# GpSimd in place of VectorE for the first rounding step of w_gate and w_val, one tile ahead

## The chip, the cores and the metric

The kernel runs on one NeuronCore of a Trainium2 chip. The metric is device time in microseconds, from the first to the last instruction of the program plus what the launch adds around it; lower is better. Five engines work side by side, each through its own queue in program order: TensorE (PE, with its weight loads as PEld), VectorE (DVE), ScalarE (ACT), GpSimd (POOL) and SyncE (SP). In this kernel SP does nothing but issue DMA transfers.

## The reference

Three steps in float32 follow one another.

```
attention: 8 batches x 8 heads, 576 tokens in chunks of 64, head size 64
           P = softmax(q k^T / 8) within a chunk;  x = P v         -> x: 4608 tokens x 512
GLU:       gate = sigmoid(x @ w_gate);  val = x @ w_val            w_gate, w_val: 512 x 1536
           y = (gate * val) @ w_out                                w_out: 1536 x 512
activation MLP: h = y @ w_in;  g = h if h >= 1, 0 if h <= -1, else (h+1)^2/4
           out = g @ w2_out                                        2048 wide inside
```

## The kernel before, in words

Every float32 product is formed from three matmuls on rounded halves: an operand is split into a high part, rounded to TensorE's `fp32r` form, and a low part, the remainder. A tile of weights therefore has to be converted and split before it can be used. The weights arrive as 64-bit words (two 32-bit words per value), and the conversion of one tile of 128 x 512 values, named by its key (`("g", 0)`, `("v", 0)`, `("g", 1)`, ...; k0, k1, k2, ... below), runs over three engines:

- `w_load` (SP, L103): the transfer from memory into the tile `raw`.
- `w_low` (L112, a `tensor_scalar` on DVE): the low words are scaled and clamped in place, the first step.
- `w_bits`: a `scalar_tensor_tensor` on DVE (L118) joins sign bits and low word; an ACT step (L122) scales the high word.
- `w_split`: `w_join` on DVE (L126), the high part on ACT (L135), and the remainder on POOL (L136, `w<-raw,w`). After that TensorE can use the tile `w`.

There are 24 tiles of this kind, k0 to k23 (`gate` and `val` in turn, 12 each). The tiles of the later weights pass through `w_low`, `w_bits` and `w_join` too, but are then combined further.

The tokens are worked through in nine blocks of 512. First comes `first_block()`: the attention of block 0, for four pairs of heads p0 to p3, with an order written out by hand in the string `ORDER`. Its letters are the steps: t (transposes of q and k), s (scores on PE at L321, row maxima and subtraction on DVE at L331 and L333, exponential on ACT at L338), n (row sums at L343 to L346 on DVE and the scaling of P on POOL, L351), p (the transpose PT of P on PE at L357 and its copy on ACT at L360), o (the product with v at L367, then x with its low part on ACT at L375 and DVE at L380), and c, which takes the next piece of weight conversion from a list named `pieces`. The loads are issued in the order of the string `LOADS`, further weight loads as pieces are done.

After that, block 0 and every later block go through the projection loop: 24 slots a block, a slot being one projection of 12 matmuls (L459 to L461, `pr<-x,w`). Around these slots the function `at(slot, priority, ...)` places all other work, and `emit(slot)` writes it into the queues in order of slot and priority. During block 0 the slots carry the conversion of the remaining weight tiles (in slot n: the split of the tile used in slot n + 4, the first and second step of the tile used in slot n + 5, the load of the tile for slot n + 9) and the attention of block 1, a new pair of heads every five slots. The first step of that attention is t, which here is two transposes on DVE (L304); its scores on PE (L321) stand one slot later. After block 0 no w_gate or w_val tile is converted any more.

Of the kernel before, what the change touches and what calls it, by code (L numbers as in the profile page):

```python
# [29 lines left out]
def kernel(  # L30
# [15 lines left out]
    nc = tc.nc  # L46
# [31 lines left out]
    def f32(t):  # L78
        return t.bitcast(F32)
# [6 lines left out]
    keys = [(kind, f) for f in range(F1) for kind in "gv"]  # L86
# [4 lines left out]
    def words(raw):  # L91
        return lambda i, dt: raw.bitcast(dt).rearrange("p (n w) -> p n w", w=2)[:, :, i]

    def w_load(key):
        kind, f = key
        sl = slice(f * P, (f + 1) * P)
        if kind in "gv" and keys.index(key) < 8:
            raw = wp.tile([P, 512], I64, tag="w", name="raw")
        else:
            raw = pool["raw"].tile([P, 512], I64, tag="raw", name="raw", bufs=pool["nraw"])  # L100
        src = {"g": w_gate, "v": w_val, "o": w_out, "i": w2_in, "p": w2_out}[kind]
        if kind in "gvi":
            nc.sync.dma_start(  # L103
                out=raw.rearrange("p (k f) -> p k f", f=P), in_=src[:, sl].rearrange("(k p) f -> p k f", p=P)
            )
        else:
            nc.sync.dma_start(out=raw, in_=src[sl, :])
        raws[key] = raw

    def w_low(key):  # L110
        word = words(raws[key])
        nc.vector.tensor_scalar(  # L112
            out=word(0, I32), in0=word(0, U32), scalar1=2.0**-29, scalar2=7.0, op0=ALU.mult, op1=ALU.min
        )

# [77 lines left out]
    def s_prep(kind, k):  # L193

        half_ = (F1 if kind == "o" else F2) // 2
        a, b = (kind, k), (kind, k + half_)
        return [
            (0, w_load, a), (0, w_load, b), (4, w_low, a), (4, w_bits, a), (5, w_low, b), (5, w_bits, b),
            (6, w_join, a), (6, w_join, b), (7, s_sums, kind, k), (8, s_split, kind, k, 0), (8, s_split, kind, k, 1),
            (9, s_split, kind, k, 2), (10, s_spool, kind, k, 0), (10, s_spool, kind, k, 1),  # L200
            (10, s_split, kind, k, 3), (11, s_spool, kind, k, 2), (12, s_spool, kind, k, 3),
        ]
# [179 lines left out]
    def first_block():  # L382
        ft = ps.tile([P, BS], F32, tag="b5", name="fill")

        def fill(n):
            for _ in range(n):
                nc.tensor.matmul(ft, lhsT=z[:, :P], rhs=z, start=True, stop=True)

        pieces = []
        for i in range(NW + 1):  # L390
            pieces.append((w_low, keys[i]))
            pieces.append((w_bits, keys[i]))
            if i:
                pieces.append((w_split, keys[i - 1]))
        nl = [0]

        def wl(n):
            for _ in range(n):
                w_load(keys[nl[0]])
                nl[0] += 1  # L400

        def conv(n):
            while n and pieces:
                fn, key = pieces.pop(0)
                fn(key)
                if fn is w_split and nl[0] < NW + 5:
                    wl(1)
                n -= fn is not w_low

        z = pool["sg"].tile([P, BS], F32R, tag="sg", name="z", bufs=4)  # L410
        nc.vector.memset(f32(z), 0.0)
        kv_["ident"] = cp.tile([P, P], F32, name="ident")
        make_identity(nc, kv_["ident"])
        a = Whole(
            0, [["b0", "b2", "b4"], "b1", "b3", "b6", "b7", "b5"],
            lambda nm: wp.tile([P, 2, BS], F32, tag="w", name=nm), "MVMT",
        )
        for c in LOADS:
            if c == "w":
                wl(1)  # L420
            elif c in "0123":
                a.load(int(c))
            else:
                a.v_load("abcd".index(c))
        for c in ORDER.split():
            if c[0] == "f":
                fill(int(c[1:]))
            elif c[0] == "c":
                conv(int(c[1:]))
            else:  # L430
                for fn in {"t": "t", "s": "sme", "n": "nw", "p": "pc", "o": "oxl"}[c[0]]:
                    getattr(a, fn)(int(c[1:]))
        conv(99)
        assert nl[0] == NW + 5, nl
# [317 lines left out]
    def at(slot, prio, fn, *args):  # L752
        order[0] += 1
        ev.setdefault(int(slot // 1), []).append((slot % 1, prio, order[0], fn, args))
# [15 lines left out]
    NW = 4  # L770
    for i, key in enumerate(keys):
        if i >= NW + 5:
            at(i - NW - 5, 2.5, w_load, key)
        if i > NW:
            at(i - NW - 1, 6, w_low, key)
            at(i - NW - 1, 6, w_bits, key)
        if i >= NW:
            at(i - NW, 5.5, w_split, key)
# [17 lines left out]
    for i in range(FIRST):  # L796
        key, name = ("o", 0, i), ("o", 0, 1, i)
# [52 lines left out]
    with tc.manual_schedule():  # L850
# [13 lines left out]
        pool["nraw"] = 8  # L864
        open_pool("u", "au")
        first_block()
        for t in range(-6, 0):
            emit(t)
# [52 lines left out]
```

## Time and profile before

| what | value |
|---|---|
| median of 3 runs | 1714.94 us (1713.28 to 1716.34) |
| the profiled execution | 1715.51 us, of it span 1713.7 us |
| PE busy in the span | 1668.6 us, 97% |
| DVE, ACT, POOL busy | 1171.4, 863.9, 833.8 us (68%, 50%, 49%) |
| conversion of w_gate and w_val | from 7.9 us (first L112) to 120.7 us (end of the last L136) |

The span is the time from the first to the last recorded instruction; the execution's own time is 1.8 us longer. A row of a timeline gives the start, the duration, engine, line, operation, written and read tiles, and in brackets how long the engine stood idle before and for whom. Rows joined by "x2" or "x32" are several equal instructions in one. A row of waits gives waiting line, the engine and line waited for, microseconds in total, number of waits, longest.

### The profile page before, as it was taken

Reading aid. Unit: us, or ns where it says so; the run is one execution under the profiler, and the core shown is the slowest. Engines: PE = TensorE matmul, PEld = TensorE weight load, DVE = VectorE, ACT = ScalarE, POOL = GpSimd, SP = SyncE. Lnnn points to the kernel's source line nnn. Section 1 sums busy time; section 2 is a strip of 40 time slices with the busy share of each in tenths; the row PEclk is TensorE's granted clock in tenths of the full one; section 3 lists DMA queues with packets and bytes.
Section 4 is the critical chain, followed back from the end, with each engine's and each line's share of the span. In section 5 each row is a group of like instructions: output and inputs, shape, how many; then the busy total and the mean of one; then the engine's idle time right before and its main releaser. Section 6 shows DMA issues by size and latency. Waiting matters only on the chain.

```text
span 1713.7 us, 29607 instructions
## 1 busy us (share of the span) xinstructions
PE 1668.6 (97%) x10658; PEld 1528.4 (89%) x10658; DVE 1171.4 (68%) x1727; ACT 863.9 (50%) x1560; POOL 833.8 (49%) x758
## 2 busy tenths in 40 slices
PE   6899999999999999999999999999999999999996
PEld 5678888888888888899999989999999999999996
DVE  5874555555555541297777767888787888887975
ACT  4664454445444541155555555555554545455542
POOL 2432444433434340177777754444350477677774
PEclk7999999999999999999999999999999999999998
DMA  8856768777668656634644653423329764455442
GB/s 203 218 134 163 213 172 239 228 201 235 212 200 230 212 188 231 217 122 141 226 142 148 246 221 133 155 104 148 148 107 340 281 215 116 107 156 154 115 111 38
DMA packets 386723, 307.11 MB, mean 179 GB/s; under 512 B 268944, under 2 KB 299664, under 8 KB 386576
## 3 DMA queue, kind: packets, MB, share of 16 engines
q1 hardware_dynamic: 386576, 305.22, 57.8%
q8 instruction: 84, 1.38, 0.3%
q14 instruction: 63, 0.52, 0.1%
HBM read 179.83 MB, written 125.30 MB: 178 GB/s over the span
## 4 chain that ended last, share of the span: by engine, by line
PE 86%; DVE 7%; SPq 2%; ACT 1%; issue 1%; POOL 1%; DMA 1%; ACTq 0%; DVEq 0%; POOLq 0%
PE P L460 17%; PE P L461 17%; PE P L459 16%; PE pr L459 11%; PE pr L461 11%; PE pr L460 11%; DVE z L492 3%; PE O L367 2%; PE S L321 1%; SPq L284 1%; DVE z L503 1%; PE PT L357 1%; POOL z L503 1%; DVE raw L118 1%; DVE raw L126 0%
## 5 line engine op out<-in xcount | busy, mean ns | idle before, releaser
L503 POOL TENSOR_TENSOR z<-z 128x384 fp32r<-128x384 f32 x308 | 357.2, 1184 | 313.3 <-ACT z L496 309.1
L460 PE MATMUL P<-z,w 128*128 128x384 f32 x1344 | 451.5, 336 | 8.4 <-DVE z L503 4.2
L459 PE MATMUL P<-z,w 128*128 128x384 f32 x1344 | 449.8, 335 | 0.8 <-ACT z L496 0.8
L461 PE MATMUL P<-z,w 128*128 128x384 f32 x1344 | 449.6, 335 | 0.0
L459 PE MATMUL pr<-x,w 128*128 128x512 f32 x864 | 347.8, 403 | 0.0
L461 PE MATMUL pr<-x,w 128*128 128x512 f32 x864 | 338.0, 391 | 0.0
L460 PE MATMUL pr<-x,w 128*128 128x512 f32 x864 | 337.4, 391 | 0.0
L496 ACT ACTIVATE z<-z 128x384 fp32r<-128x384 f32 x420 | 205.1, 522 | 180.3 <-DVE z L492 105.8
L878 DVE TENSOR_TENSOR sg<-pr,sg 128x512 f32<-128x512 f32 x108 | 74.6, 691 | 313.0 <-PE pr L461 144.5
L460 PEld LDWEIGHTS P<-z,w 128*128 128x128 f32 x1344 | 252.8, 188 | 13.6 <-POOL z L503 7.7
L503 POOL TENSOR_TENSOR op<-in,op 128x384 fp32r<-128x384 f32 x168 | 190.8, 1155 | 148.2 <-ACT op L496 147.8
L459 PEld LDWEIGHTS P<-z,w 128*128 128x128 f32 x1344 | 252.7, 188 | 1.3 <-ACT z L496 1.1
L461 PEld LDWEIGHTS P<-z,w 128*128 128x128 f32 x1344 | 252.8, 188 | 0.0
L459 PEld LDWEIGHTS pr<-x,w 128*128 128x128 f32 x864 | 162.6, 188 | 35.4
L461 PEld LDWEIGHTS pr<-x,w 128*128 128x128 f32 x864 | 162.5, 188 | 35.3
L460 PEld LDWEIGHTS pr<-x,w 128*128 128x128 f32 x864 | 163.0, 189 | 31.4
L496 ACT ACTIVATE op<-in 128x384 fp32r<-128x384 f32 x252 | 128.5, 524 | 112.8 <-PE P L461 60.7
L875 ACT ACTIVATE sg<-pr 128x512 f32<-128x512 f32 x108 | 64.5, 597 | 233.5 <-PE pr L461 226.7
L492 DVE TENSOR_TENSOR z<-z 128x384 f32<-128x384 f32 x200 | 169.9, 900 | 5.8 <-POOL z L503 5.8
L460 PE MATMUL P<-op,w 128*128 128x384 f32 x504 | 168.5, 334 | 0.1
L459 PE MATMUL P<-op,w 128*128 128x384 f32 x504 | 168.4, 334 | 0.0
L461 PE MATMUL P<-op,w 128*128 128x384 f32 x504 | 168.4, 334 | 0.0
(63 smaller groups left out, 2250.0 us busy)
## 6 DMA issues: line engine op xcount, KB each, us to landing
uT<-ua SPq DMA_DIRECT2D x96, 384.0 KB, 2.3
z<-uT SPq DMA_DIRECT2D x96, 384.0 KB, 4.2
gT<-sg SPq DMA_DIRECT2D x108, 256.0 KB, 2.4
in<-gT SPq DMA_DIRECT2D x72, 256.0 KB, 4.0
raw<-in_moe_w_out_dram SPq DMA_DIRECT2D x28, 512.0 KB, 5.3
w<-swi SPq DMA_DIRECT2D x28, 512.0 KB, 6.1
w<-swp SPq DMA_DIRECT2D x28, 512.0 KB, 6.8
swi<-st SPq DMA_DIRECT2D x24, 512.0 KB, 4.0
```

Source lines behind the costliest of these rows:

```text
L118: nc.vector.scalar_tensor_tensor(out=word(0, I32), in0=word(1, I32), scalar=-(2**31), in1=word(0, I32), op0=ALU.bitwise_and, op1=ALU.bitwi ...
L284: nc.sync.dma_start(out=t[32 * g:32 * g + 32, i], in_=rows[h, :, 32 * j:32 * j + 32].rearrange("(t i) r -> i t r", i=32),)
L321: nc.tensor.matmul(banks[h][heads[c % 2], c // 2], lhsT=t[hs, 0, ts], rhs=t[hs, 1, ts], start=True, stop=True)
L367: nc.tensor.matmul(banks[h][hs, ts], lhsT=self.V[p][hs, c], rhs=self.SP[p][hs, 1, ts], start=True, stop=True)
L459: nc.tensor.matmul(o, lhsT=ah, rhs=bh, start=first, stop=False, skip_group_check=open_)
L460: nc.tensor.matmul(o, lhsT=ah, rhs=bl, start=False, stop=False, skip_group_check=open_)
L461: nc.tensor.matmul(o, lhsT=al, rhs=bh, start=False, stop=last, skip_group_check=open_)
L492: (eng or nc.vector).tensor_tensor(out=op_src(p, key), in0=x, in1=y, op=ALU.subtract)
L496: nc.scalar.activation(o[:, 0], op_src(p, key), AF.Copy)
L503: eng.tensor_tensor(out=o[:, 1], in0=op_src(p, key), in1=f32(o[:, 0]), op=ALU.subtract)
L875: nc.scalar.activation(sg, go, AF.Sigmoid)
L878: nc.vector.tensor_tensor(out=sg, in0=vo, in1=sg, op=ALU.mult)
```

## The change

For keys of w_gate and w_val, `w_low` runs on GpSimd; for all other weights it stays on VectorE. In both places where it is issued it comes earlier by one tile: in the list `pieces` of `first_block()` the first step of tile i + 1 stands ahead of the second step of tile i, and in the slots of block 0 the first step is placed one slot before the second. Nothing else differs. Line numbers of the changed kernel are higher by one from L113 on (L113 for L112, L137 for L136, L352 for L351), and by two from L393 on.

```diff
     def w_low(key):
         word = words(raws[key])
-        nc.vector.tensor_scalar(
+        eng = nc.gpsimd if key[0] in "gv" else nc.vector
+        eng.tensor_scalar(
             out=word(0, I32), in0=word(0, U32), scalar1=2.0**-29, scalar2=7.0, op0=ALU.mult, op1=ALU.min
         )
...
         for i in range(NW + 1):
-            pieces.append((w_low, keys[i]))
+            for j in ([0, 1] if i == 0 else [i + 1] if i < NW else []):
+                pieces.append((w_low, keys[j]))
             pieces.append((w_bits, keys[i]))
...
         if i > NW:
-            at(i - NW - 1, 6, w_low, key)
+            at(i - NW - 2, 6, w_low, key)
             at(i - NW - 1, 6, w_bits, key)
```

The queues of PE, ACT and SP hold the same instructions in the same order as before. On DVE 24 instructions go, on POOL 24 come. At the start POOL's queue was as follows (before; `raw_127`, `_141`, `_143`, `_156` and `_164` are k0 to k4, the `sp` tiles are p0 to p3 in turn):

```order
masks.py:199 AFFINE_SELECT ident_119<-ident_119 128x128
L351 TENSOR_TENSOR sp_195<-sp_195,r_247 128x512
L136 TENSOR_TENSOR w_276<-raw_127,w_276 128x512
L351 TENSOR_TENSOR sp_250<-sp_250,r_293 128x512
L351 TENSOR_TENSOR sp_296<-sp_296,r_337 128x512
L351 TENSOR_TENSOR sp_369<-sp_369,r_420 128x512
L136 TENSOR_TENSOR w_432<-raw_141,w_432 128x512
```

In the changed kernel the same stretch of POOL's queue reads:

```order
L113 TENSOR_SCALAR raw_127<-raw_127 128x512
L113 TENSOR_SCALAR raw_141<-raw_141 128x512
L113 TENSOR_SCALAR raw_143<-raw_143 128x512
L352 TENSOR_TENSOR sp_196<-sp_196,r_248 128x512
L137 TENSOR_TENSOR w_277<-raw_127,w_277 128x512
L113 TENSOR_SCALAR raw_156<-raw_156 128x512
L352 TENSOR_TENSOR sp_251<-sp_251,r_294 128x512
L352 TENSOR_TENSOR sp_297<-sp_297,r_338 128x512
L352 TENSOR_TENSOR sp_370<-sp_370,r_421 128x512
L137 TENSOR_TENSOR w_433<-raw_141,w_433 128x512
```

The first step of k2 now stands ahead of the scaling of p0, and that of k3 ahead of the scalings of p1, p2 and p3. From slot 0 on POOL's queue alternates, where before it held L136 after L136 (changed kernel; `raw_164`, `_166`, `_280`, `_436`, `_474` are k4 to k8):

```order
L113 TENSOR_SCALAR raw_166<-raw_166 128x512
L137 TENSOR_TENSOR w_530<-raw_164,w_530 128x512
L113 TENSOR_SCALAR raw_280<-raw_280 128x512
L137 TENSOR_TENSOR w_585<-raw_166,w_585 128x512
L113 TENSOR_SCALAR raw_436<-raw_436 128x512
L137 TENSOR_TENSOR w_614<-raw_280,w_614 128x512
L113 TENSOR_SCALAR raw_474<-raw_474 128x512
L352 TENSOR_TENSOR sp_563<-sp_563,r_641 128x512
```

The first step of tile k(i+2) now stands right behind the remainder of tile k(i) and ahead of that of k(i+1). On DVE the same stretch was, before (the two rows of `raw_166` are k5's):

```order
L304 STREAM_TRANSPOSE qkT_525<-qk_505 128x512 x2
L126 SCALAR_TENSOR_TENSOR raw_164<-raw_164 128x512
L112 TENSOR_SCALAR raw_166<-raw_166 128x512
L118 SCALAR_TENSOR_TENSOR raw_166<-raw_166 128x512
L126 SCALAR_TENSOR_TENSOR raw_166<-raw_166 128x512
L112 TENSOR_SCALAR raw_279<-raw_279 128x512
L118 SCALAR_TENSOR_TENSOR raw_279<-raw_279 128x512
```

In the changed kernel the two rows of L112 are gone from it, and all else stands as it was.

## Rows read from the trace of the kernel before

**Rows 1.** The page: busy time of the engines, share, instructions.
```profile
PE 1668.6 (97%) x10658; PEld 1528.4 (89%) x10658; DVE 1171.4 (68%) x1727; ACT 863.9 (50%) x1560; POOL 833.8 (49%) x758
```
**Rows 2.** Waits of PE, 39 to 125 us: total, times, longest.
```profile
PE S L321 <- DVE qkT L304: 8.9, 4, 3.1
```
**Rows 3.** Waits of PE after 125 us, the largest.
```profile
PE P L460 <- DVE z L503: 4.2, 3, 1.8
```
**Rows 4.** Windows: length, busy PE, PEld, DVE, ACT, POOL, clock, DMA share, GB/s.
```profile
0.00:39.00 39.00, 24.91 (x346) 20.93 (x346) 22.05 (x50) 19.32 (x28) 7.83 (x12) 0.72 0.88 213
39.00:125.00 86.00, 76.94 (x580) 60.98 (x580) 73.24 (x125) 57.10 (x83) 35.39 (x26) 0.97 0.71 179
```
**Rows 5.** Timeline of PE: the four scores of block 1 that waited.
```profile
44.55 0.64 PE L321 MATMUL S<-qkT 64*64 64x64 f32 x28 [1.68 <-DVE qkT L304]
...
62.45 0.69 PE L321 MATMUL S<-qkT 64*64 64x64 f32 x32 [2.53 <-DVE qkT L304]
82.17 1.13 PE L321 MATMUL S<-qkT 64*64 64x64 f32 x32 [3.15 <-DVE qkT L304]
101.35 0.69 PE L321 MATMUL S<-qkT 64*64 64x64 f32 x32 [1.50 <-DVE qkT L304]
```
**Rows 6.** The source line L112 up to 125 us: ns min/median/max.
```profile
L112 DVE TENSOR_SCALAR raw<-raw x24: 416/424/1272, 7.9 to 114.9; 128x512 int32<-128x512 uint32 x24
```
**Rows 7.** Groups of POOL by form: busy, mean ns, idle before.
```profile
L136 POOL TENSOR_TENSOR w<-raw,w 128x512 fp32r<-128x512 f32 x24 | 33.1, 1379 | 43.5 <-ACT w L135 37.5 <-DMA qk<-in_k_dram 3.9 <-DMA qk<-in_q_dram 2.1
...
masks.py:199 POOL TENSOR_SCALAR_AFFINE_SELECT ident<-ident 128x128 f32<-128x128 f32 x1 | 0.3, 295 | 0.1
```
**Rows 8.** SP's issue of the load of k3, and its landing.
```profile
L103 SPq DMA_DIRECT2D raw<-in_moe_w_val_dram x1: 623/623/623, 20.3 to 20.3; - x1
...
DMA to landing us min/median/max: 6.5/6.5/6.5
```
**Rows 9.** Timeline of POOL in the first block: remainder of k0, scaling of p1.
```profile
20.28 1.43 POOL L136 TENSOR_TENSOR w<-raw,w 128x512 fp32r<-128x512 f32 x1 [1.49 <-ACT w L135]
22.06 1.04 POOL L351 TENSOR_TENSOR sp<-sp,r 128x512 f32<-128x512 f32 x1 [0.34 <-DVE r L346]
```
**Rows 10.** Timeline of PE in the first block: PT of p1, S of p3, O of p1.
```profile
23.93 0.65 PE L357 MATMUL PT<-ident,sp 128*128 128x128 f32 x4
25.87 0.79 PE L321 MATMUL S<-qkT 64*64 64x64 f32 x32 [1.29 <-ACT qkT L313]
27.52 2.17 PE L367 MATMUL O<-sp,vd 64*64 64x64 f32 x32 [0.86 <-ACT sp L360]
```
**Rows 11.** Timeline of DVE in slots 0, 1 and 3 of block 0.
```profile
44.42 1.48 DVE L126 SCALAR_TENSOR_TENSOR raw<-raw 128x512 int32<-128x512 int32 x1
45.82 0.42 DVE L112 TENSOR_SCALAR raw<-raw 128x512 int32<-128x512 uint32 x1
46.28 0.69 DVE L118 SCALAR_TENSOR_TENSOR raw<-raw 128x512 int32<-128x512 int32 x1
47.71 0.99 DVE L126 SCALAR_TENSOR_TENSOR raw<-raw 128x512 int32<-128x512 int32 x1 [0.74 <-ACT raw L122]
...
55.47 1.27 DVE L112 TENSOR_SCALAR raw<-raw 128x512 int32<-128x512 uint32 x1
56.77 1.82 DVE L118 SCALAR_TENSOR_TENSOR raw<-raw 128x512 int32<-128x512 int32 x1
```
**Rows 12.** Timeline of POOL in the same stretch.
```profile
44.06 1.30 POOL L136 TENSOR_TENSOR w<-raw,w 128x512 fp32r<-128x512 f32 x1 [3.10 <-ACT w L135]
46.70 1.46 POOL L136 TENSOR_TENSOR w<-raw,w 128x512 fp32r<-128x512 f32 x1 [1.34 <-ACT w L135]
...
55.07 1.38 POOL L351 TENSOR_TENSOR sp<-sp,r 128x512 f32<-128x512 f32 x1 [0.41 <-DVE r L346]
56.74 1.30 POOL L136 TENSOR_TENSOR w<-raw,w 128x512 fp32r<-128x512 f32 x1 [0.28 <-ACT w L135]
```
**Rows 13.** Timeline of ACT: the high part of k4.
```profile
45.94 0.69 ACT L135 ACTIVATE w<-raw 128x512 fp32r<-128x512 f32 x1 [1.96 <-DVE raw L126]
```

## The prediction

> **What bounds the kernel now.** I read the page first: PE is busy 97% of the span [rows 1], so a change on DVE and POOL can only move the 3% in which PE waits. The waits of PE, cut into stretches, say where that is. After 125 us no wait named is longer in total than 4.2 us [rows 3], and the changed instructions are over by then. From 39 to 125 us, while block 0 is projected, PE waits 8.9 us, all of it for one line: the scores of block 1 (L321) wait for DVE's transposes (L304), four times [rows 2]. The timeline shows the four: 1.68, 2.53, 3.15 and 1.50 us [rows 5]. The window says why: there DVE is busy 73.24 of 86 us, POOL 35.39, ACT 57.10 [rows 4]. DVE's queue runs late there, and the transposes stand in it behind the weight conversion. Before 39 us PE is busy 24.91 of 39 us [rows 4]: loads and the chain of block 0's attention.
>
> So 8.9 us (0.52%) is the most that relief of DVE can bring, and whatever delays the first four transposes costs its full length.
>
> **What the change takes from DVE.** 24 instructions of 0.42 us go [rows 6], all but the first few after 39 us. Three slots of one kind gain more: in slots 3, 8 and 13 L112 stands behind the scaling of P on POOL. In slot 3 it began at 55.47 and took 1.27, ending 0.29 after L351's end (55.07 + 1.38 = 56.45); L118 behind it began at 56.77 and took 1.82, ending 0.55 after the end of L136 (56.74 + 1.30 = 58.04) [rows 11, 12]. That is a lock: an instruction of DVE with two inputs in SBUF (L118, L126), or L112 itself, stands until the POOL instruction under way is over, then runs its 0.55 us or 0.3 us; it can slip in between two POOL instructions that follow on each other, as L112 did here.
>
> **What it adds on POOL.** The trace has no first step on POOL. Bounds of its length x: from below the 0.42 us on DVE [rows 6]; from above the 1.38 us of L136, same size and stride but two inputs [rows 7]. The nearest row with one input is the affine select of 128 values, 0.295 us [rows 7]; with a fixed part of 0.1 us (my estimate) that is 1.5 ns a value, so 0.87 us for 512. I take x = 0.87.
>
> The Trainium skill (GPSIMD Engine Reference, Performance versus the Vector engine) measures 769 ns for 512 values in a tight loop with one input; by that estimate the cases below would shift towards the short x. No run shown here has such an instruction.
>
> **The first block: a new wait.** POOL's queue now holds the first step of k3 ahead of the scalings of p1, p2 and p3. The load of k3 is issued at 20.28 and lands 6.5 us later, at 26.8 [rows 8]. POOL is free from 21.7 [rows 9] and stands until 26.8 + 0.87 = 27.65, with p1 behind it, which was ready at 22.06 [rows 9]. The scaling of p1 takes 1.04, so PT of p1 starts at 28.75 instead of 23.93. PT was early: O of p1 only began at 27.52 [rows 10]. But in PE's queue PT and S of p3 (0.65 and 0.79) stand ahead of O, so O of p1 begins at 30.2, 2.7 us late, or 3.2 if both run slowly after PE's longer idle time, as the score at 82.17 did (1.13 instead of 0.69) [rows 5]. From there to the first transpose nothing gives way: O, x, softmax of p3, O of p3, x of p3, L118, L126, L304 follow on each other. One L112 stood among the last of these, so 0.43 comes back. First transpose and first score late by 2.3 to 2.8: **+2.5 us**. PE's own projections shift with it, so the 1.68 us wait stays.
>
> **Block 0: the lock eats the relief.** POOL's work per slot rises from L136 alone to L136 plus x, back to back, and every L118 and L126 can fall on it. At slot 0, with times unshifted: L126 of k4 waits for the remainder of k3 (44.06 + 1.30 = 45.36) and ends at 45.90 [rows 11, 12]. POOL's first step of k5 gets the lock then and ends at 45.90 + 0.87 = 46.77. L118 of k5 needs it, so it is ready at about 46.8 (it began at 46.28 before). The remainder of k4 is ready at 46.70, as ACT's part ends at 46.63 [rows 12, 13], so it goes first and holds L118 until 48.07; L118 ends at 48.6 instead of 46.97, 1.65 late. ACT's step and L126 of k5 follow: 0.74 of waiting [rows 11], then POOL's next first step in the way; about 0.9 us of it remains one slot on. With x under 0.75 us L118 goes first, and the slot costs 0.1 or nothing. At 0.87 it is close to a toss-up.
>
> In the softmax slot (3, 8, 13) L118 now waits only for L351: it ends at 56.45 + 0.55 = 57.0 instead of 58.59, 1.6 us earlier, or 1.0 if POOL's first step has pushed L351 back by 0.6.
>
> A period of five slots therefore runs from -0.8 (no race lost) to +2.0 us (two or three lost) at x = 0.87. Walked in the same way, the first period comes to +0.3 to +2.0 and the two after it to -0.8 to 0 each, since there ACT's own queue, not DVE's, sets part of the pace: together **+0.5 us**, from -1.1 to +2.0. What PE waits at L321 moves by as much, one to one. After the fourth score (101.35) PE waits for nothing up to 125 us [rows 2, 5], so the few first steps that are left (the last at 114.9 [rows 6]) are covered by PE's work; without that cover each would be worth 0.42 us of DVE or x of POOL.
>
> **Sum.** +2.5 + 0.5 = +3.0 us. The profiled execution took 1715.51 us (span 1713.7 and 1.81 around it), so 1718.5 on its basis; it lies 0.57 above the median of 1714.94, on which I forecast 1718.0, within 1716.3 to 1719.7.
>
> The Trainium skill (SBUF — State Buffer, Who interferes with whom) states the lock as a rule: a VectorE instruction with two SBUF inputs and any GpSimd instruction that reads SBUF exclude each other for the whole instruction. The rows above agree for POOL with two inputs (L118, 1.82 us instead of 0.69); by the rule it holds with one input as well, which speaks against the second rival below.
>
> **Rivals.**
> *POOL's first step is slow (x up to 1.38), slower than before.* Then every race like the one at 46.70 is lost: L118 of k5 would end at 45.90 + 1.38 + 1.30 + 0.55 = 49.1, 2.1 late, 1.4 of it lasting. Periods of +1 to +3 us and a first block of +3.0 give +6 to +12: 1721 to 1727, about 1723. For it: the shortest POOL instruction of 512 values shown takes 1.04 us (L351 [rows 9]), and the step converts integers on the way. Against: one input, not two. It decides from x of about 1.1 us.
>
> *No lock with one input, faster.* Then DVE gains 0.45 us a slot and about 0.85 more in the softmax slot, 3.1 a period, enough to take away the waits of 2.53, 3.15 and 1.50. The first-block delay of 2.5 stays; slower PE after the long wait (the score at 82.17 took 1.13 instead of 0.69 [rows 5]) gives back about 0.8. -7.2 + 2.5 - 0.8 = -5.5: 1709.5. Against it: L112 itself has one input and was locked out by L351.
>
> *Short x (about 0.55) with the lock.* No race is lost, softmax slots gain: three periods give -0.65, -1.5, -1.5, the first block +2.2. Sum -1.4: 1713.5. It needs x below 0.75.
>
> **Numbers.** This kernel's runs tell 0.2% from no change, which is 3.4 us: above 1718.4 or below 1711.5. Forecast case 0.48, of it 0.27 below 1718.4 and 0.21 above, since it lies at the border; slow step 0.22, slower; no lock 0.17, faster; short step with lock 0.13, same. Faster 0.17, same 0.40, slower 0.43. The range runs from 1710 to 1723.5, leaving out about half of either outer case (0.2 together); the likeliest case alone spans 1716.3 to 1719.7.
>
> **What would show it.** (1) On POOL, a first step that starts at about 26.8 us with idle time put down to a load, and the scaling of p1 near 27.7. (2) PE's first projection matmul 2.5 us or so later. (3) The mean of the 24 POOL instructions: 0.87, and which side of 0.75 and 1.1. (4) L118 and L126 lengthened to between 1 and 2 us in more slots than before, ending 0.55 after a POOL end. (5) The waits of L321 for L304 in total near 8.9 + 0.5. After 125 us nothing should differ. I am wrong if p1's scaling starts before 24 us, if O of p1 keeps its time, or if L118 runs inside POOL's first step without getting longer.

## The result and the profile after: 20 us slower

The changed kernel takes 1734.48 us in the median of 4 runs (1731.52 to 1735.29), the kernel before 1714.37 us in the runs beside it: a ratio of 1.0113, with an interval of 1.0095 to 1.013, or 20 us more. The forecast was 1718.0 with a range from 1710 to 1723.5. The direction leaned the right way (slower 0.43 against same 0.40); the size was far off.

The page of the changed kernel, busy time of the engines (answers to [rows 1]):

```profile
span 1733.1 us, 29607 instructions
PE 1675.4 (97%) x10658; PEld 1533.5 (88%) x10658; DVE 1159.4 (67%) x1703; ACT 864.4 (50%) x1560; POOL 892.9 (52%) x782
```

POOL has 59.1 us more than before, DVE 12.0 less. For 24 instructions that is some 2.5 us each on POOL, with what its other instructions were lengthened by; the forecast had 0.87 for the first step. PE's busy time grew too, from 1668.6 to 1675.4 us for the same 10658 instructions: of the 19.4 us by which the span is longer, 6.8 are PE working more slowly and 12.6 are PE standing. (Profiles of kernels below that run at the time of before have 1665.3 to 1671.4 us of busy time, so this split holds to some 3 us.) The instruction by itself, from the view of its source line (ns minimum, median, maximum):

```profile
L113 POOL TENSOR_SCALAR raw<-raw x24: 1967/2144/2507, 7.2 to 128.2; 128x512 int32<-128x512 uint32 x24
```

Even the shortest takes 1.97 us, over the upper bound of 1.38 that the forecast had set.

Waits of PE from 39 to 136 us; the conversion of w_gate and w_val now ends at 137.7 us (total, times, longest; answers to [rows 2]):

```profile
PE PT L358 <- POOL sp L352: 11.7, 4, 5.3
PE S L322 <- DVE qkT L305: 6.0, 4, 2.6
PE O L368 <- ACT sp L361: 1.3, 2, 0.7
```

Before, PE waited only for the transposes; now most of its waiting is for POOL's scaling of P. The window over the same stretch as in [rows 4] (busy PE, PEld, DVE, ACT, POOL, clock, DMA share, GB/s):

```profile
0.00:39.00 39.00, 22.39 (x314) 19.25 (x314) 19.04 (x43) 18.01 (x25) 15.62 (x16) 0.84 0.88 214
39.00:125.00 86.00, 69.26 (x490) 54.22 (x489) 53.91 (x88) 47.19 (x69) 77.90 (x42) 0.87 0.62 161
```

POOL went from 35.39 to 77.90 busy of 86 us, DVE from 73.24 to 53.91. DVE was relieved as intended; POOL is nearly always busy. The mean granted clock of PE fell from 0.97 to 0.87 of full speed, a mean of the two levels 1.0 (2.4 GHz) and 0.5 (1.2 GHz). From 61 to 67 us, for instance, it was 0.50. PE had stood for 5.26 us up to 63.77, for POOL's scaling, and most of its projections up to 67 us took 0.63 us each, where they took 0.39 before that wait. Stretches of this kind make PE's busy time longer.

The four scores of block 1 in PE's timeline, and behind them the first two of block 2, show where the time is lost (answers to [rows 5]):

```profile
46.70 0.69 PE L322 MATMUL S<-qkT 64*64 64x64 f32 x32 [0.95 <-DVE qkT L305]
...
69.59 0.69 PE L322 MATMUL S<-qkT 64*64 64x64 f32 x32 [0.67 <-DVE qkT L305]
...
93.45 0.69 PE L322 MATMUL S<-qkT 64*64 64x64 f32 x32 [1.78 <-DVE qkT L305]
...
115.06 1.00 PE L322 MATMUL S<-qkT 64*64 64x64 f32 x32 [2.64 <-DVE qkT L305]
...
132.77 1.13 PE L322 MATMUL S<-qkT 64*64 64x64 f32 x32
...
153.04 0.69 PE L322 MATMUL S<-qkT 64*64 64x64 f32 x32
```

The four stand 2.15, 7.14, 11.28 and 13.71 us later than before. The first score of block 2 stands at 132.77 instead of 115.08, 17.7 later, the second at 153.04 instead of 134.06, 19.0 later, and the span is 19.4 longer: nearly all of it is lost by the second score of block 2. After that the waits of PE are much as before.

How POOL spends two slots, from its timeline in the changed kernel, and DVE beside it:

```profile
69.48 2.38 POOL L113 TENSOR_SCALAR raw<-raw 128x512 int32<-128x512 uint32 x1
71.94 1.82 POOL L137 TENSOR_TENSOR w<-raw,w 128x512 fp32r<-128x512 f32 x1
73.84 2.31 POOL L113 TENSOR_SCALAR raw<-raw 128x512 int32<-128x512 uint32 x1
76.23 1.82 POOL L137 TENSOR_TENSOR w<-raw,w 128x512 fp32r<-128x512 f32 x1
```

```profile
71.89 0.69 DVE L119 SCALAR_TENSOR_TENSOR raw<-raw 128x512 int32<-128x512 int32 x1 [1.88 <-POOL raw L113]
72.50 0.68 DVE L880 TENSOR_TENSOR sg<-pr,sg 128x512 f32<-128x512 f32 x1
73.33 0.97 DVE L127 SCALAR_TENSOR_TENSOR raw<-raw 128x512 int32<-128x512 int32 x1
76.18 0.69 DVE L119 SCALAR_TENSOR_TENSOR raw<-raw 128x512 int32<-128x512 int32 x1 [1.87 <-POOL raw L113]
```

POOL never rests: from one L137 to the next are 76.23 - 71.94 = 4.29 us. PE's work for a slot is about 3.3 us (15.4 to 17.7 in five slots between the scores, without its waits, in [rows 5]). DVE stands 1.9 us for each first step, and the moment it is released its L119 runs against L137, which takes 1.82 instead of 1.30. From 45 to 130 us the 19 first steps take 41.8 us (4.4 of them above 1.97 each), the 19 remainders 33.1 (8.4 above 1.30 each), and the three scalings that fall into this stretch 4.2: 79.1 of 85 us.

### The profile page after: what moved, and what is told of

It is laid out like the page before. It is cut to its first block, busy times and chain, and to the rows that moved or that the text cites. A ratio compares the mean times of both kernels' runs of the same rounds, so it can differ in the third digit from the quotient of the medians.

```text
span 1733.1 us, 29607 instructions
## 1 busy us (share of the span) xinstructions
PE 1675.4 (97%) x10658; PEld 1533.5 (88%) x10658; DVE 1159.4 (67%) x1703; ACT 864.4 (50%) x1560; POOL 892.9 (52%) x782
## 3 DMA queue, kind: packets, MB, share of 16 engines
q8 instruction: 84, 1.38, 0.3%
## 4 chain that ended last, share of the span: by engine, by line
PE 84%; DVE 6%; POOL 4%; SPq 2%; issue 1%; DMA 1%; ACT 1%; ACTq 0%; DVEq 0%; POOLq 0%
PE P L462 17%; PE P L463 16%; PE P L461 16%; PE pr L461 11%; PE pr L463 10%; PE pr L462 10%; DVE z L494 3%; PE O L368 2%; POOL raw L113 2%; POOL w L137 1%; PE S L322 1%; DVE z L505 1%; SPq L285 1%; PE PT L358 1%; POOL z L505 1%
```

## The experiments

Two theories stood against each other. The first: POOL is full, because its first step is more than twice as long as forecast. The second: the order or the latency is at fault, that is, the earlier place in a queue, or DVE standing in its own queue for something asked of POOL one slot before. Each run was compared with the kernel before on the same chip.

**p1_probe: the length by itself.** Six POOL instructions on a scratch tile at the start of the kernel before, while POOL is idle.

```diff
+        for o_, i_, two in (
+            (pw(0, I32), pw(0, U32), True), (flat(I32), flat(U32), True), (pw(0, F32), pw(0, F32), True),
+            (flat(F32), flat(F32), True), (pw(0, I32), pw(0, U32), False), (flat(F32), flat(F32), False),
+        ):
...
+                nc.gpsimd.tensor_scalar(out=o_, in0=i_, scalar1=2.0**-29, scalar2=7.0, op0=ALU.mult, op1=ALU.min)
...
+                nc.gpsimd.tensor_scalar(out=o_, in0=i_, scalar1=2.0**-29, scalar2=None, op0=ALU.mult)
```

> The kernel before, with six extra POOL instructions on a scratch tile at the start, while POOL is idle, to measure the disputed length by itself: the first step as in the change (unsigned to signed integer, every second word), the same on neighbouring words, the same two operations in float32 with and without the step, and one operation instead of two. The changed kernel's own took 1.97 us when undisturbed. If the integer conversions make it long, the float32 forms take 0.9 us or less; if the step of two words does, the neighbouring ones take under 1.4; if the two operations do, the one-operation forms take under 1.2; if all tensor_scalar instructions of POOL are long, every form is within 0.3 us of 1.97.

POOL's timeline of the probe, in the order of the list (the fourth, neighbouring float32 words, is a row of the same kind at 8.58, 1.92 us):

```profile
2.27 1.98 POOL L424 TENSOR_SCALAR probe<-probe 128x512 int32<-128x512 uint32 x1
4.34 1.92 POOL L424 TENSOR_SCALAR probe<-probe 128x512 int32<-128x512 uint32 x1
6.34 2.16 POOL L424 TENSOR_SCALAR probe<-probe 128x512 f32<-128x512 f32 x1
...
10.59 1.55 POOL L426 TENSOR_SCALAR probe<-probe 128x512 int32<-128x512 uint32 x1
12.22 1.49 POOL L426 TENSOR_SCALAR probe<-probe 128x512 f32<-128x512 f32 x1
```

Neither the integers nor the step of two words explains the length (they change it by 0.24 us at most): with two operations every form takes 1.92 to 2.16 us, with one 1.49 to 1.55. The starts are as far apart as the durations say (2.07, 2.00, 2.24, 2.01, 1.63), so these lengths can be trusted. Of the expectations only the last comes near, and in part: all `tensor_scalar` forms of POOL are long here, and the second operation is 0.4 of it. Why POOL takes longer for one input with one operation (1.49 us) than for L136's two inputs (1.30 to 1.46 in [rows 12]) stays open.

**e1_order: the order alone.** The change, with the first step on DVE.

```diff
-        eng = nc.gpsimd if key[0] in "gv" else nc.vector
+        eng = nc.vector
```

> The change's order alone, with the first step still on DVE. If POOL's length is the cause of the 20 us, this runs at the time of before, 1714.4 within 2.5 us. If the earlier place in the queue is the cause (a wait for a load ahead of the attention's work), it is slower by 2.5 us or more, since DVE then waits for k3 at 26.8 us in place of POOL.

1716.99 us against 1715.75: ratio 1.0007 (0.9997 to 1.0016). At most 2.7 us come from the order; it is not the cause of 20.

**e2_first and e3_slots: the two halves.** In the first, POOL takes only k0 to k4 and the slots are as before; in the second the first block is as before and POOL takes k5 to k23, one slot ahead.

```diff
-        eng = nc.gpsimd if key[0] in "gv" else nc.vector
+        eng = nc.gpsimd if key in keys[:NW + 1] else nc.vector      # e2_first
+        eng = nc.gpsimd if key in keys[NW + 1:] else nc.vector      # e3_slots
```

> POOL takes the first step of the five tiles of the first block only, the slots are as before. If the first block's part is the wait for the load of k3 in POOL's queue, the first score of block 1 starts near 46.7 us as in the changed kernel, and the time is 2 to 3 us above before, 1716.5 to 1717.5. If the first block's delay is absorbed later, 1714.4 within 1 us. If it is most of the 20 us, over 1724.

> The first block as before, POOL takes the first step from k5 on, one slot ahead. If POOL is full in the slots (2.0 us and more plus 1.3 to 1.8 per slot, 4.3 against 3.1 that PE needs), this carries nearly all: 1729 to 1733, with POOL over 88% busy from 45 to 125 us. If the two parts act together only, under 1724.

e2_first: 1715.88 against 1715.75, ratio 1.0002 (0.9992 to 1.0011). e3_slots: 1732.32, ratio 1.0098 (1.0083 to 1.0113), 16.8 us more. So the slots carry nearly all. The wait in the first block is there; in POOL's timeline of e2_first the first step of k3 stands for its load, and two scalings stand behind it:

```profile
25.45 1.97 POOL L113 TENSOR_SCALAR raw<-raw 128x512 int32<-128x512 uint32 x1 [2.41 <-DMA raw<-in_moe_w_val_dram]
27.50 2.04 POOL L352 TENSOR_TENSOR sp<-sp,r 128x512 f32<-128x512 f32 x2
```

Its first score of block 1 stands at 46.73 us, where the one profile of before has 44.55. The other kept profiles bear out the wait, not a price: with the changed first block and POOL at work in it, the scaling of p1 starts at 25.70 to 28.42 us and the first score at 43.66 to 46.74; with the first block as before, at 21.75 to 23.56 and at 43.37 to 45.68. But the time does not show 2 us: the interval reaches from 1.4 under to 1.9 over before. Whether those 2 us are given back, or were partly chance of one profile (the runs of before range over 5 us on this chip), stays open.

**e4_half, e6_half_lead and e5_lead: how full, and how far ahead.** In e4_half POOL takes every second first step (the w_val tiles from k5 on), one slot ahead, with the first block as before; in e6_half_lead the same, two slots ahead; e5_lead is the changed kernel with all of them two slots ahead.

```diff
-        eng = nc.gpsimd if key[0] in "gv" else nc.vector
+        eng = nc.gpsimd if key in keys[NW + 1:] and key[0] == "v" else nc.vector     # e4_half, e6_half_lead
...
-            at(i - NW - 2, 6, w_low, key)
+            at(i - NW - (2 if key[0] == "v" else 1), 6, w_low, key)     # e4_half
+            at(i - NW - (3 if key[0] == "v" else 1), 6, w_low, key)     # e6_half_lead
+            at(i - NW - 3, 6, w_low, key)                               # e5_lead
```

> From k5 on POOL takes the first step of the w_val tiles only, every second slot; w_gate and the first block stay as before. If a full POOL is the cause, it isn't full here (per period of five slots 5 x 1.38 + 1.3 + 2.5 x 2.0 = 13.2 us, some 15 with blocked time, against 16 to 19): within 3 us of before, and no wait of the transposed probabilities (PT) for POOL. If the cost goes with the number of instructions moved (each one makes VectorE wait in its queue for POOL), half of the 16.6 us is left: 8 us over before.

> As e4_half (POOL takes the first step of w_val tiles from k5 on; 4.4 us over before), but two slots ahead. If those 4.4 us are VectorE standing for a first step that was asked for one slot before (11.4 us of such waits in e4_half), they go: within 2 us of before. If they are POOL's queue itself, 3 to 5 us stay.

> The changed kernel with the first step two slots ahead instead of one in the slots. If a full POOL is the cause, more lead changes nothing: within 3 us of the changed kernel's 1734. If latency is (VectorE standing for a result that is asked for one slot ahead), most of it goes: under 1724.

| kernel | us | before beside it | ratio (interval) | POOL busy of 45 to 125 us |
|---|---|---|---|---|
| e4_half | 1719.84 | 1715.46 | 1.0029 (1.0018 to 1.0041) | 57.58 |
| e6_half_lead | 1715.96 | 1715.6 | 1.0004 (0.9995 to 1.0013) | 56.10 |
| e5_lead | 1728.01 | 1715.46 | 1.0077 (1.0059 to 1.0094) | 75.79 |

Both theories hold a part. POOL is far from full in e4_half, and it still costs 4 to 5 us (0.29%). The waits of DVE for POOL from 39 to 140 us in e4_half and then in e6_half_lead:

```profile
DVE raw L119 <- POOL raw L113: 11.4, 8, 1.9
```

```profile
DVE raw L119 <- POOL raw L113: 1.9, 1, 1.9
```

With two slots of lead the standing goes and the cost with it. In e5_lead, where POOL is as full as in e3_slots (75.79 and 75.15 of 80 us), the same lead gives back some 6 of the 20 us and leaves 13.2. By one profile of each, PE's named waits up to 136 us are as long as in the changed kernel (19.1 against 19.0 us), and what is less is PE's busy time, 1669.6 instead of 1675.4. Lead alone does not make up for an engine without room. The expectation that latency would explain most of the 20 us, and mine that it explains nothing of it, are both wrong.

**x_short192 and x_short352: the length turned down.** The changed kernel with POOL's first step over 192 or 352 of the 512 columns. What is left out: the low bits of w_gate and w_val do not enter their values.

```diff
+        nc_ = 192 if key[0] in "gv" else 512
...
-            out=word(0, I32), in0=word(0, U32), scalar1=2.0**-29, scalar2=7.0, op0=ALU.mult, op1=ALU.min
+            out=word(0, I32)[:, :nc_], in0=word(0, U32)[:, :nc_], scalar1=2.0**-29, scalar2=7.0, op0=ALU.mult, op1=ALU.min
...
-            op0=ALU.bitwise_and, op1=ALU.bitwise_or,
+            op0=ALU.bitwise_and, op1=ALU.bitwise_and if key[0] in "gv" else ALU.bitwise_or,
```

> The changed kernel, but POOL's first step covers only 192 of the 512 columns, and the second step of w_gate and w_val drops the low bits (a bitwise and in place of the or), so that the step is short, 0.8 to 1.0 us. This is the length on which the forecast stood. If a full POOL is the cause, the 16 us are gone. If the forecast's lock counts (a POOL instruction with one input holds up VectorE's L118 and L126 for its whole length), 2 to 5 us over before; without it 2 to 6 us under before.

> As x_short192 with 352 columns, 1.3 to 1.5 us, the length of the forecast's slow rival. Full POOL: 1.30 + 1.4 + 0.16 between them + 0.67 of blocked time = 3.5 us a slot, 19 slots and 5 us of scalings are 72 us, about what the stage took before (43 to 117): 0 to 5 us over before. The forecast's walk for this length said 6 to 12.

The lengths, one row from the tile view of each kernel:

```profile
L114 POOL TENSOR_SCALAR raw<-raw x24: 867/888/1402, 7.6 to 112.1; 128x192 int32<-128x192 uint32 x24
```

```profile
L114 POOL TENSOR_SCALAR raw<-raw x24: 1417/1453/1956, 7.9 to 117.1; 128x352 int32<-128x352 uint32 x24
```

x_short192 takes 1715.06 us against 1715.6, ratio 0.9999 (0.9990 to 1.0009); x_short352 takes 1723.34, ratio 1.0047 (1.0032 to 1.0062), 8 us more. Everything but the length is as in the changed kernel (the second step on DVE keeps its 0.69 us), so the length is the cause: nothing at 0.87 us, 8 at 1.42, 20 at 1.97. At 1.42 POOL is not full either (67.08 of 80 us busy from 45 to 125), so a sum of POOL's busy time alone, which gave 0 to 5, is too kind; DVE stands 18.1 us for first steps there. But DVE's standing is not the price by itself either: x_short192 has 10.7 us of it, nearly as much as e4_half with 11.4, and loses no time. How much of each stand reaches PE, no run here tells apart. The rival "POOL's first step is slow" had said 6 to 12 for this length.

**t1_early, w1_both, w2_copy: is there a gain to be had?** t1_early is the kernel before with the transposes of block 1 one slot earlier; w1_both adds that to e6_half_lead; w2_copy is w1_both with ACT's copy of the transposed probabilities half a slot ahead as well.

```diff
-    later_block(1, [5 * p for p in range(KT)], (0, 1, 1.5, 2, 3, 3, 5, 5.5, 7, 7.5, 8))
+    later_block(1, [5 * p for p in range(KT)], (-1, 1, 1.5, 2, 3, 3, 5, 5.5, 7, 7.5, 8))     # t1_early, w1_both
+    later_block(1, [5 * p for p in range(KT)], (-1, 1, 1.5, 2, 3, 3, 5, 5, 7, 7.5, 8))       # w2_copy
```

> The kernel before, with the transposes of block 1 (L304) one slot earlier in VectorE's queue and nothing on POOL. If PE's waits of 8.9 us there come only from the place of the transposes in a queue that runs late, most of three of them go (7.2 us) and the first (which hangs on the first block) stays: 5 to 7 us under before. If VectorE's amount of work is the limit, PE waits for something else of VectorE later in the period (x, the probabilities or a weight tile): within 2 us of before.

> e6_half_lead (POOL takes every second first step from k5 on, two slots ahead) with the transposes of block 1 one slot earlier. If a wait on one path was hidden behind the other's (transposes late in one kernel, probabilities late in the other), the two together gain what neither did: 3 to 6 us under before. If ScalarE's copy of the probabilities, late in t1_early, sets the pace by itself, within 2 us of before.

> As w1_both, and ScalarE's copy of the transposed probabilities (L361) stands ahead of the weight steps of its slot instead of behind them. If that copy is what PE waited for in t1_early (5.8 us), those waits go too: 4 to 8 us under before, and under w1_both. If the copy then holds up the weight steps, no better than w1_both.

No gain: 1715.7 against 1715.46 (1.0001, 0.9991 to 1.0010), 1718.19 against 1714.96 (1.0017, 1.0008 to 1.0026) and 1718.41 (1.0025, 1.0014 to 1.0036); the last two are 3 and 4 us slower than before. The waits of PE from 39 to 160 us in t1_early show what took the place of the old ones:

```profile
PE O L367 <- ACT sp L360: 5.8, 3, 2.4
PE S L321 <- DVE qkT L304: 2.5, 2, 2.3
PE PT L357 <- POOL sp L351: 0.9, 1, 0.9
```

The 8.9 us of waiting for the transposes fell to 2.5, and 6.7 us of other waits came up behind them. In w2_copy the wait for the copy is gone, and PE waits 8.3 us for POOL's scaling, against 4.7 in w1_both. No version here beats the kernel before.

## Why the prediction was wrong

*What bounds the kernel: right in where, incomplete in what.* Nearly all that moved (19.0 of 19.4 us) lies before the second score of block 2. No version tried here gained any of the 8.9 us: t1_early shows that the wait that PE names there covers others of nearly the same size. And for a slower PE the forecast allowed under 1 us (0.5 in the first block's range, 0.8 in one rival), where it is about 6.8 of the 19.4 us.

*The length x = 0.87 us, "from above the 1.38 us of L136, same size and stride but two inputs": this is the step that failed.* It measured 1.97 us at least and 2.14 in the median. The rows gave no ground for the upper bound: none showed that two inputs must cost more than one. And the affine select from which I scaled is another operation, with 128 values; the fixed part of 0.1 us was in no row. In place of 0.1 us and 1.5 ns a value the runs show 0.2 us and 3.4 ns a column. What an operation costs on an engine where the trace does not show it is not bounded by a different operation of the same size. The Trainium skill (GPSIMD Engine Reference, Performance versus the Vector engine) gives 769 ns for 512 values as the best case of a tight loop. The probe's instructions took 1.49 to 2.16 us, so they do not reach that best case, and it was no price for them.

*The first block, +2.5 us: the mechanism is shown, its price is not.* The first step of k3 started at 26.35 us (forecast 26.8) and the scaling of p1 at 28.42 (27.65); the first score was 2.15 late in the profile, but e2_first's time lies from 1.4 us under to 1.9 over before, which leaves no room for the whole 2.5.

*Block 0, "the lock eats the relief", +0.5 us: wrong in size with the wrong length, and in two assumptions.* With the length of the forecast, x_short192 lies 1.7 us under to 1.5 over before, where the sum had +3.0. First, the race that the walk called a toss-up was never lost: DVE's second step starts some 0.05 us ahead of POOL's remainder and keeps its 0.69 us, and the remainder is held up instead (71.89 against 71.94 above). No remainder holds up a second step in the changed kernel or in x_short192, from 43 to 136 us; the two that are long in each, 1.53 us, stood behind a scaling. In x_short192, DVE and then POOL:

```profile
47.22 0.69 DVE L120 SCALAR_TENSOR_TENSOR raw<-raw 128x512 int32<-128x512 int32 x1 [0.77 <-POOL raw L114]
```

```profile
47.27 1.81 POOL L138 TENSOR_TENSOR w<-raw,w 128x512 fp32r<-128x512 f32 x1
```

Second, the walk had POOL's first step hold up DVE's instructions with two inputs for its whole length. From the timelines of e6_half_lead, POOL and then DVE:

```profile
50.03 2.30 POOL L113 TENSOR_SCALAR raw<-raw 128x512 int32<-128x512 uint32 x1
```

```profile
50.43 0.85 DVE L113 TENSOR_SCALAR raw<-raw 128x512 int32<-128x512 uint32 x1
51.31 0.69 DVE L119 SCALAR_TENSOR_TENSOR raw<-raw 128x512 int32<-128x512 int32 x1
```

L119 runs in the middle of POOL's L113 (50.03 to 52.33) at its undisturbed 0.69; in this kernel it does so seven times. (DVE's own L113, with one input, took 0.85 there instead of 0.42.) Held up is rather POOL: by the two figures above 1.97 and 1.30, its first steps and remainders lost up to 12.8 us to DVE from 45 to 130 us of the changed kernel. I had priced only the other side of the lock.

*The rivals.* "POOL's first step is slow" was the right one in kind, with 0.22; its own bound of 1.38 us kept it from 20 us. At 1.42 us, x_short352 shows its 6 to 12 (8 measured), but that is in part luck: it counted on lost races, and there too no remainder holds up a second step. What the forecast's own case added to "slower" (0.21 of the 0.43) hung on the first block's price and on the same races, and no time shows either. "No lock with one input" was right in that L119 runs inside the first step, and wrong about the gain: in x_short192 PE's waits for the transposes fell from 8.9 to 4.5 us, 3.3 us of waits for POOL's scaling came in, and the time stayed. "Short x" and the forecast's length came out alike, at no change.

*The range.* It took in the bounds of x, and the upper one, 1.38, was 0.59 us short of the shortest measured. With 1.97 us for x, POOL alone needs 1.97 + 1.30 = 3.27 us a slot, as much as PE's 3.3, before the 12.8 / 19 = 0.67 us that it loses to DVE. With the right length the walk would have found POOL all but full; POOL's side of the lock and PE's clock would still have been missing.

## What to carry to other kernels

Before work is moved to an idle engine, its length there has to be measured, or the range has to reach well past the nearest rows: here the length was 1.4 times the longest of them (1.97 against 1.38 us) and 4.7 times that on DVE (0.42). The share of idle time says nothing until the length is known. Work for a second engine that sits in the first one's chain needs room and lead both: half the work two slots ahead cost nothing, half the work one slot ahead 4 to 5 us, all of it 13 to 20. And a wait that PE names first may hide others of its size: moving the transposes took away 6.4 us of waits for them, and no time.

## What the runs showed of the hardware

- A `tensor_scalar` on GpSimd over 128 x 512 words takes 1.92 to 2.16 us with two operations and 1.49 to 1.55 with one, for integers and float32, with a step of one word or two (p1_probe); DVE takes 0.42 for the form with two operations [rows 6]. With two operations it grows evenly with the columns: 0.87, 1.42 and 1.97 us at the least for 192, 352 and 512 (x_short192, x_short352, the changed kernel), or 3.4 ns a column and 0.2 us besides.
- The lock between DVE and GpSimd is seen with POOL's two-input instructions (L118 in [rows 11, 12]). With the one-input first step L119 kept its 0.69 us in the midst of it (e6_half_lead). The Trainium skill (SBUF — State Buffer, Who interferes with whom) has a VectorE instruction with two SBUF inputs contend with a GpSimd instruction that reads SBUF, the second of the two blocked for the whole of the first. For a one-input first step that is already under way these rows disagree; in the other order, in the next point, they agree.
- POOL's first step is lengthened by what DVE has under way at its start. Of the 19 from 45 to 130 us of the changed kernel, the 11 that start while an L127 of DVE is under way take 2.30 to 2.51 us (73.84 above); the other eight take 1.97 to 1.99, although in four of them an L127 runs from start to end.
